# A linear-attention block and an MLP on one core: other zero products, another engine for the finest level of the first two tiles, 128 weight columns at three levels of the first tile, and another order

## The chip, the cores and the metric

The kernel runs on 1 core of one Trainium2 chip. The metric is the device time of one execution in microseconds. Three executions of the kernel before took 588.12, 589.46 and 591.12 us; the median is 589.46. One more execution was profiled; it took 589.61 us, of which the trace spans 587.8. All durations below are from that one.

## The reference

The attention is a recurrence over time with a decay per channel; its output, laid out as tokens by channels, goes through an MLP with the exact gelu.

```python
# r, k, v, w: (4, 8, 768, 48), u: (8, 48)
for t in range(S):
    cur = np.einsum('bhd,bhe->bhde', u[None] * kt, vt)
    y[:, :, t] = np.einsum('bhd,bhde->bhe', rt, state + cur)
    state = wt[:, :, :, None] * state + np.einsum('bhd,bhe->bhde', kt, vt)
x = y.transpose(0, 2, 1, 3).reshape(3072, 384)
h = x @ w_in                      # (384, 2048)
out = (0.5 * h * (1.0 + erf(h / sqrt(2)))) @ w_out   # (2048, 384)
```

Activations are 32-bit floats; the two weight matrices arrive as 64-bit floats.

## The kernel before

**Tiles.** The work is cut into 8 tiles x = 0 to 7: four batches by two halves of 384 time steps. A tile has all 8 heads, two to a slot of the partitions (g = 0, 1, 64 partitions each, 48 used). `attention(x, unit)` makes a tile's xT (channels by 384 steps), `mlp(x)` turns it into output rows. Tile 0's attention runs as two parts (units, np_ = 1) that alternate; later tiles have one. The loads of r, k, w (`rkw`) and v of a tile come by SP's queue.

**Inside a chunk of 64 steps** the attention needs the 64x64 matrix of k·r products with the decays between the two times. It is built in `a_sb` (k's time on partitions, r's time along the row, chunks c = 0, 1 on the two halves of the partitions) by levels h = 1, 2, 4, 8, 16, 32. At level h the products of a later block of h steps with the block of h steps before it are valid. Tiles 0 and 1 do it with `halves()`, tiles 2 to 7 with `quarters()`, which the diff does not touch. In `halves()`, for each h:

- `products` (L443 to L456) fills a pair of PSUM banks `d` by PE, with 64x64 weights on four 64x64 tiles of the array, 24 matmuls (each 2 records in the trace, and 2 of PEld) in a part of tile 0, 48 in tile 1. In tile 0 two products of zeros, 128x128 by 512, follow (`keep_warm(2)`).
- At h = 1 the diagonal's products with u·r (`diagonal`, in `kx` by ACT, L401) come next.
- DVE multiplies r and k by the decays for the next level (L494 in separate halves, L505 in one instruction). It needs that level's products done, since it overwrites their input.
- The result goes from `d` to the places of `a_sb` where the level is valid: for h below 16 by DVE's COPY_PREDICATED with a mask (L516), for h = 16 and 32 by ACT copies of blocks of 16 or 32 rows (L513). At h = 1 DVE then copies the diagonal by a mask (`copy_diagonal`, L465).

There are three pairs of banks `d`, so a product of a later level waits until an earlier pair has been copied.

**Then** k is transposed (kt_ps L685, copied by ACT L687), k·v per chunk (kv_ps L711), DVE chains the states (L731, L726), PE adds to y the part inside the chunk (L752) and that of the states (L797), with a small DVE copy between them (`fence`, L762 and L764), and DVE and ACT copy y to xT (L804, L820, and over `ysb` L823 and DMAs L827).

**MLP.** Tile 0's MLP has 16 column blocks of three 128x384 matmuls (L1059) with gelu by ACT in two banks, and then the products with w_out (L1153). Tiles 1 to 7 use a form with sums of blocks (L929, L1073), and POOL issues adding DMAs there (L980).

**Weights** come in 16 pieces of 64-bit numbers (`raw`, five buffers) and are turned to 32 bits by three ACT passes (L333, L334, L336) and two DVE instructions, a shift (L345) and an add (L349). The first MLP's block pair n needs piece n. `weight_in` issues a piece's load; some loads are held back until DVE has done a one-element memset of their target (L204, and L163 for tile 1's r, k, w).

**Order.** Nothing is scheduled by a tool: each part of the work is a generator, and the strings in `PLAN` say, letter by letter, which generator runs to its next yield. Engines execute their own instructions in the order in which this issues them. In `PLAN[0]` "." and "s" are the two parts of tile 0, "f" is tile 1's attention, "c" the weights' conversion, "l" loads. In `PLAN[x]` "." is the MLP of tile x - 1, "s" and "f" the attentions of tiles x and x + 1.

At the start `keep_warm(8)` (L225) issues eight products of zeros while the first loads run, and masks for h = 1, 2, 4, 8 and the diagonal are made by DVE.

Of the kernel before, what the change touches and what calls it, by code (L numbers as in the profile page):

```python
# [10 lines left out]
F32 = mybir.dt.float32  # L11
# [17 lines left out]
NI = Q * N3  # L29
LEVELS = (1, 2, 4, 8, 16, 32)  # L30
QUARTERS = (4, 16)
FINE = 4
BANK = 512
# [3 lines left out]
NC_SP = 8  # L37
HALFWAY = 2
PLAN = {
    0: "l.s....llsl.lssslslss.lc.l.slslls...ssss..lcs.s.s.l.ss..ss..sccs.c.s.llpssslw..cs.ffpcc",  # L40
    1: (
        "..ccswccc.csl.scscs.s.sccwsc.clccs.ccsccc.csc.lscclswwclc.scs.wcssw.ss.cclcsc.ccs.lclccsc."
        "ccclfccccccfccfcccccfccfccwf.ff......fw.sl.w.x.wx...x..x...xww"
    ),
    2: (
        "s.s.....ss....ssw.ws.wl.wsss.wws.s..lsl...lws.w..s.ww....s.s..l..sss.lssss....s..s..s.sls."
        "llsf.sf.fs..fl.xx.x.fxx"
    ),
    3: (
        "ls.ls....lss..ss.....ss..l.s.lsss.sss.s.s.s.ss..sss..sssssss....s.s..l...s..l.sslslsf.ffs."  # L50
        "..x.lx..xxx"
    ),
    4: (
        "lls.s.sss..s.l.........ssss.....sss.s.ss.s..s.sllss...s.s..l.sss.ss..s.ss...s..sslsll.s..f"
        ".sf.sf..ff..xx.xflxx"
    ),
    5: (
        "..ss...s..ssl....sls...s.sss..sss..sss.sls...sllss..sssss.s..l..s.s...s.slll..s.ssfsf.fsf."
        "....xxx.lxx"
    ),  # L60
    6: (
        "ss..sss...s.....s.sl..s...l.s.ssls.s.s..s..sssssl......ss.ssss.sl.sl...s.....ss..llsssl.f."
        "s.fsf.f.f.xx.l.xffxx"
    ),
    7: "....ss.s...s.s.s....s.sss..ss.ss.sss..s..sss..sssssss......s.s....s..ssss.s...x.x..xxx",
}


# [5 lines left out]
def kernel(  # L74
# [31 lines left out]
    def pair(name):  # L106
        return pools["d"].tile([128, 2, BANK], F32, name=name, tag="d")
# [116 lines left out]
        for _ in range(n):  # L224
            nc.tensor.matmul(t, lhsT=zeros[:, 0:128], rhs=zeros, start=True, stop=True)  # L225

    keep_warm(8)


    masks = {h: const.tile([128, C // 2], U8, name=f"mask{h}") for h in LEVELS if h < 16}  # L230
# [9 lines left out]
    for h in masks:  # L240
        if not h:
            continue
        sh = h.bit_length() - 1
        s_h = s_qs.get(h, s_t)
        nc.vector.tensor_scalar(out=s_h, in0=row, scalar1=sh, scalar2=None, op0=ALU.logical_shift_right)
        nc.vector.tensor_scalar(out=m_h[:, 0:C // 2], in0=col[:, 0:C // 2], scalar1=sh, scalar2=1,
                                op0=ALU.logical_shift_right, op1=ALU.logical_shift_left)
        nc.vector.tensor_tensor(out=masks[h], in0=s_h[:, 0:C // 2], in1=m_h[:, 0:C // 2], op=ALU.is_equal)
# [58 lines left out]
    def conversion():  # L307

        i = converted[0]
        if i >= len(pieces):  # L310
            return
        converted[0] += 1

        prepare(i + HALFWAY if i > 1 else 0)
        yield
        if wide:
            yield from finish(pieces[i][0], raws[i], *halfway[i])
        for _ in weight_in(i + 3):
            pass

    def convert():
        for _ in conversion():
# [30 lines left out]
    def attention(x, unit):  # L353
# [91 lines left out]
        def products(bs, right, width, rest=False):  # L445
            d = pair("d")
            n = 0
            for b in bs:
                for i in range(NI):
                    for g in range(2):  # L450
                        for p in range(2):
                            nc.tensor.matmul(d[half[p], g, n * width:(n + 1) * width],  # L452
                                             lhsT=kc[half[g], b, i, p], rhs=right(half[g], b, i, p),
                                             start=True, stop=True)
# [14 lines left out]
        def halves():  # L469

            for h in LEVELS:
                m = C // 2 // h
                if np_ < NPART:

                    d = products(range(np_), lambda z, b, i, p: rc[z, b, i, p], C, h == 1)
                    d = d.rearrange("p g (n m two j) -> p g n m two j", two=2, j=h, m=m)[:, :, :, :, 1, :]
                else:
                    right = rc.rearrange("p b i c (m two j) -> p b i c m two j", two=2, j=h)[:, :, :, :, :, 1, :]
                    d = products(range(np_), lambda z, b, i, p: right[z, b, i, p], C // 2)
                    d = d.rearrange("p g (n m j) -> p g n m j", j=h, m=m)  # L480
# [10 lines left out]
                tt = bass.AP(tensor=t2.tensor, offset=t2.offset, ap=[t2.ap[0], [1, 2]] + list(t2.ap[1:]))  # L491

                def update(z, r2=r2, t2=t2, k2=k2, tk=tk):
                    nc.vector.tensor_mul(*((k2, k2, tk) if z is k else (r2, r2, t2)))  # L494

                if x == 0 and m == 1:

                    update(k)
                    last_r.append(lambda: update(r))
                elif x == 0 and h == 1:  # L500
                    update(r)
                    yield
                    update(k)
                else:
                    nc.vector.tensor_mul(rk, rk, tt)  # L505
                yield
                ah = at.rearrange("p g n (m two j) -> p g n m two j", two=2, j=h)[:, :, :, :, 1, :]
                if h >= 16:

                    for p in range(2):  # L510
                        for i in range(m):
                            s = slice(p * 64 + i * 2 * h, p * 64 + i * 2 * h + h)
                            nc.scalar.copy(out=ah[s, :, :, i], in_=d[s, :, :, i])  # L513
                else:
                    mask = masks[h].rearrange("p (m j) -> p m j", j=h).unsqueeze(1).unsqueeze(1)
                    nc.vector.copy_predicated(out=ah, mask=mask.to_broadcast(ah.shape), data=d)  # L516
                if h == 1:
                    copy_diagonal(diag)
                yield
# [798 lines left out]
```

## Time and profile before

| what | value |
|---|---|
| median of three executions | 589.46 us |
| profiled execution | 589.61 us, span 587.8 us |
| PE busy | 571.1 us, 97% of the span |
| DVE busy | 425.5 us, 72% |
| ACT busy | 291.2 us, 50% |
| POOL busy | 58.6 us, 10% |
| first MLP matmul of tile 0 (L1059) starts | 44.40 us |
| output products of tile 0 done, banks of tiles 1 to 7 set up (L115) | 118.36 us |

The span begins with the first instruction. "PE" rows are matmuls, "PEld" the loads of their weights. A row of the timeline gives start, length, engine, line, operation, output and input, how many instructions were merged, and in brackets the idle time before and what ended it; "issue" means that nothing the profile shows was waited for. A busy PE is not a PE at its peak: matmuls are pipelined, and a row of merged matmuls holds the last one's whole latency.

### The profile page before, as it was taken

The page shows a single profiled execution, that of the slowest core. Times are in us where ns is not written, and L with a number is a line of the kernel's source. Part 1 is how long each engine was busy: PE and PEld are TensorE (multiplying, and loading weights), DVE is VectorE, ACT ScalarE, POOL GpSimd, SP SyncE. Part 2 cuts the span into 40 slices and gives each one's busy share as a digit, 9 for nine tenths or more (in the row PEclk, how much of TensorE's full clock was granted, in tenths as well). Part 3 has the DMA queues.
Part 4 walks back from the last instruction along what each step waited for, and adds up shares of the span by engine and source line. Part 5 has one row for each costly group of instructions (what it writes and reads, how often), then busy time and mean ns, then how long its engine had stood idle before and what let it go on. Part 6 is the DMA issues. An engine that isn't in the chain of part 4 may idle for free. (4 is left out here: it accounts for less than half of the span.)

```text
span 587.8 us, 17656 instructions
## 1 busy us (share of the span) xinstructions
PE 571.1 (97%) x7602; PEld 521.4 (89%) x7616; DVE 425.5 (72%) x825; ACT 291.2 (50%) x668; POOL 58.6 (10%) x63
## 2 busy tenths in 40 slices
PE   5789999999999999999999999999999999999997
PEld 3576666799999999999999999999998999999997
DVE  5988968989758975777959986777759987420332
ACT  2368898446362567235462467245561467335400
POOL 3100000013000130012000130002100111003100
PEclk8999999999999999999999999999999999999999
DMA  6749742253032542354122632344224333114201
GB/s 230 221 135 352 265 168 78 79 142 52 5 89 64 157 58 41 90 142 93 26 55 79 151 70 44 86 139 74 27 41 119 86 42 42 29 45 55 28 13 35
DMA packets 62430, 55.09 MB, mean 94 GB/s; under 512 B 32400, under 2 KB 47504, under 8 KB 62352
## 3 DMA queue, kind: packets, MB, share of 16 engines
q1 hardware_dynamic: 50832, 45.62, 25.5%
q0 software_dynamic: 11424, 8.26, 10.8%
q8 instruction: 60, 0.98, 0.7%
q14 instruction: 18, 0.15, 0.1%
q10 hardware_dynamic: 96, 0.07, 0.1%
HBM read 36.24 MB, written 4.72 MB: 70 GB/s over the span
## 5 line engine op out<-in xcount | busy, mean ns | idle before, releaser
L929 PE MATMUL h_ps<-xT,w_in_sb 128*128 128x192 f32 x560 | 111.5, 330 | 0.6 <-DVE o_sb L1196 0.6
L980 POOL DMA_DIRECT2D g<-o_sb x42 | 50.6, 1229 | 478.2 <-ACT o_sb L965 468.9
L929 PEld LDWEIGHTS h_ps<-xT,w_in_sb 128*128 128x128 f32 x560 | 93.0, 190 | 4.7 <-ACT g L961 1.6
L929 PE MATMUL u_ps<-s,w_in_sb 128*128 128x192 f32 x224 | 41.2, 327 | 0.0
L1073 PE MATMUL o_ps<-w_out_sb,g 128*128 128x192 f32 x224 | 39.8, 326 | 0.0
L929 PEld LDWEIGHTS u_ps<-s,w_in_sb 128*128 128x128 f32 x224 | 37.1, 190 | 0.2
L1073 PEld LDWEIGHTS o_ps<-w_out_sb,g 128*128 128x128 f32 x224 | 37.0, 190 | 0.0
L604 ACT COPY a_sb<-d 32x256 f32<-32x256 f32 (+8 forms) x90 | 32.6, 362 | 4.9 <-PE d L588 3.4
L1059 PE MATMUL h_ps<-xT,w_in_sb 128*128 128x384 f32 x96 | 33.2, 494 | 0.0
L452 PEld LDWEIGHTS d<-rkw 64*64 64x64 f32 x1152 | 19.4, 138 | 14.7 <-issue 10.5
L1073 PE MATMUL o_ps<-w_out_sb,f 128*128 128x192 f32 x176 | 32.0, 331 | 0.0
L1073 PE MATMUL o_ps<-t,g 128*128 128x192 f32 x176 | 31.4, 330 | 0.0
L1073 PE MATMUL o_ps<-t,s 128*128 128x192 f32 x176 | 31.2, 328 | 0.0
L1073 PE MATMUL o_ps<-t,e 128*128 128x192 f32 x176 | 30.6, 326 | 0.5 <-issue 0.5
L621 DVE COPY_PREDICATED a_sb<-quarter,d 128x480 f32<-128x480 uint8 (+5 forms) x54 | 23.2, 439 | 10.5 <-PE d L588 9.3
L726 DVE SCALAR_TENSOR_TENSOR st<-st,tot_sb,kv_ps 128x48 f32<-128x48 f32 x160 | 28.9, 258 | 2.6 <-PE kv_ps L711 2.5
L1073 PE MATMUL o_ps<-w_out_sb,e 128*128 128x192 f32 x176 | 30.7, 328 | 0.0
L982 DVE TENSOR_TENSOR g<-g,o_sb 128x384 f32<-128x384 f32 x14 | 7.6, 549 | 31.2 <-ACT o_sb L965 31.1
L1073 PEld LDWEIGHTS o_ps<-t,e 128*128 128x128 f32 x176 | 28.9, 190 | 0.7 <-issue 0.7
L1073 PEld LDWEIGHTS o_ps<-t,g 128*128 128x128 f32 x176 | 28.6, 190 | 0.5
L1073 PEld LDWEIGHTS o_ps<-w_out_sb,f 128*128 128x128 f32 x176 | 28.5, 190 | 0.6
L1073 PEld LDWEIGHTS o_ps<-t,s 128*128 128x128 f32 x176 | 28.8, 190 | 0.2
(163 smaller groups left out, 1171.3 us busy)
## 6 DMA issues: line engine op xcount, KB each, us to landing
rkw<-in_rkw_dram SPq DMA_DIRECT2D x54, 256.0 KB, 3.6
g<-o_sb POOLq DMA_DIRECT2D x42, 192.0 KB, 3.6
raw<-in_w_out_dram SPq DMA_DIRECT2D x8, 768.0 KB, 6.2
v_in<-in_v_dram SPq DMA_DIRECT2D x8, 584.0 KB, 4.6
raw<-in_w_in_dram SPq DMA_DIRECT2D x5, 768.0 KB, 7.5
out_dram<-o_sb SPq DMA_DIRECT2D x20, 192.0 KB, 2.0
rkw<-kx SPq DMA_DIRECT2D x72, 48.0 KB, 2.0
rkw<-in_rkw_dram SPq DMA_DIRECT2D x6, 384.0 KB, 6.2
```

The lines of the kernel that those rows point to most:

```text
L452: nc.tensor.matmul(d[half[p], g, n * width:(n + 1) * width], lhsT=kc[half[g], b, i, p], rhs=right(half[g], b, i, p), start=True, stop=True)
L604: nc.scalar.copy(out=at[z, g, first:behind, (a + 1) * h:], in_=d[z, :, :, to] if g == slice(None) else d[z, :, to])
L621: nc.vector.copy_predicated(out=an[:, :, :, :, (a + 1) * h:], mask=mask.to_broadcast(data.shape), data=data)
L726: nc.vector.scalar_tensor_tensor(out=stq[:, q, c], in0=stq[:, q, c - 1] if c else b4[:, q, NC - 1], scalar=totq[:, q, c:c + 1], in1=kvs[q ...
L929: nc.tensor.matmul(o, lhsT=lhsT, rhs=rhs, start=start, stop=True, skip_group_check=True)
L980: nc.gpsimd.dma_start(out=g, in_=z, accum_op=ALU.add)
L982: nc.vector.tensor_add(g, g, z)
L1059: nc.tensor.matmul(h_ps, lhsT=w_in_sb[:, f // FI, j, f % FI * 128:(f % FI + 1) * 128], rhs=xT[:, j, :], start=(j == 0), stop=(j == NJ - 1))
L1073: nc.tensor.matmul(o, lhsT=lhs(j), rhs=rhs(j), start=start and j == 0, stop=(j == HF - 1), skip_group_check=True)
```

## The change

Five edits.

1. The opening burst of zero products goes from 8 to 24.
2. The two zero products after each set of tile 0 become four on 64x64 tiles, each with 512 columns (`keep_warm_tiles`).
3. In tile 0, levels 1, 16 and 32 use `products_of_both`: weights of both chunks of a pair side by side, 64 rows by 128 columns, and as moving data the later blocks of both chunks, 64 columns. 12 matmuls take the place of 24; half of the result is used.
4. At h = 1, in tiles 0 and 1, ACT copies the products to all odd columns of `a_sb` (two copies of 64x384 per part of tile 0, one of 128x768 in tile 1), and POOL sets those with k's time after r's to zero by two affine selects of 64 partitions (384 columns in tile 0, 768 in tile 1). DVE's mask for h = 1 and its COPY_PREDICATED are gone. The coarser levels overwrite the rest.
5. All strings of `PLAN` are other strings. Weight piece 3 is loaded beside piece 4 after the second conversion, where it was loaded after the first.

In the order that results, the load of the first third of weight piece 0 is released after DVE's first update of r instead of before the first loads have landed. In tile 0 one part's transposes stand before the other part's products of h = 32, the shift of weight piece 0 before the updates of h = 8 and its add before the last update, and the shift of piece 1 before the last fence. In tile 1 the MLP matmuls of tile 0 between the products of successive steps, from h = 1's diagonal to h = 2, 4, 8, 16, 32 and the transposes, are 9, 6, 3, 3, 6 and 3, where they were 6, 6, 6, 6, 6 and 3. PE's instructions of tiles 1 to 7 are the same in number and shape.

```diff
 PLAN = {
-    0: "l.s....llsl.lssslslss.lc.l.slslls...ssss..lcs.s.s.l.ss..ss..sccs.c.s.llpssslw..cs.ffpcc",
+    0: ".s...ls.lsl.l.sslsls.ls.s..llcss.lclslsc.slsslcl..ls.ss.sc.lss...s.sp...sscs.wc.ss.ccfpf",
...
-    keep_warm(8)
+    def keep_warm_tiles():
+        ts = [ps.tile([128, BANK], F32, name="warm", tag="mm", bufs=2) for _ in range(2)]
+        for p in range(2):
+            for g in range(2):
+                nc.tensor.matmul(ts[g][half[p]], lhsT=zeros[half[g], 0:64], rhs=zeros[half[g]], start=True, stop=True)
+
+    keep_warm(24)
...
-        for _ in weight_in(i + 3):
-            pass
+        for n in (() if i == 0 else (3, 4) if i == 1 else (i + 3,)):
+            for _ in weight_in(n):
+                pass
...
             if x == 0 and not rest:
-                keep_warm(2)
+                keep_warm_tiles()
             return d[:, :, 0:n * width]
+
+        def products_of_both(h):
+            odd = rc.rearrange("p b i c (m two j) -> p b i c m two j", two=2, j=h)[:, :, :, :, :, 1, :]
+            d = pair("d")
+            for i in range(NI):
+                for g in range(2):
+                    nc.tensor.matmul(d[:, g, i * C:(i + 1) * C], lhsT=kc[half[g], 0, i].rearrange("p c t -> p (c t)"),
+                                     rhs=odd[half[g], 0, i], start=True, stop=True)
+            keep_warm_tiles()
+            return d[:, :, 0:NI * C].rearrange("p g (n c m j) -> p g n c m j", c=2, j=h, m=C // 2 // h)
...
-                if np_ < NPART:
+                if x == 0 and (h >= 16 or h == 1):
+                    d = products_of_both(h)
+                elif np_ < NPART:
...
+                if h == 1:
+                    if x == 0:
+                        for p in range(2):
+                            nc.scalar.copy(out=ah[half[p]], in_=d[half[p], :, :, p])
+                    else:
+                        nc.scalar.copy(out=ah, in_=d)
+                    for z in half:
+                        a1 = ah[z, :, :, :, 0]
+                        nc.gpsimd.affine_select(out=a1, in_=a1, pattern=[[0, 2], [0, a1.shape[2]], [2, m]], base=1,
+                                                channel_multiplier=-1, compare_op=ALU.is_ge, fill=0.0)
...
-                            nc.scalar.copy(out=ah[s, :, :, i], in_=d[s, :, :, i])
-                else:
+                            nc.scalar.copy(out=ah[s, :, :, i], in_=d[s, :, :, p, i] if x == 0 else d[s, :, :, i])
+                elif h > 1:
                     mask = masks[h].rearrange("p (m j) -> p m j", j=h).unsqueeze(1).unsqueeze(1)
                     nc.vector.copy_predicated(out=ah, mask=mask.to_broadcast(ah.shape), data=d)
```

More of the change, by code (lines that the diff above doesn't have):

```diff
@@ L225, in keep_warm @@
             nc.tensor.matmul(t, lhsT=zeros[:, 0:128], rhs=zeros, start=True, stop=True)
-    keep_warm(8)
-    masks = {h: const.tile([128, C // 2], U8, name=f"mask{h}") for h in LEVELS if h < 16}
+    def keep_warm_tiles():
[4 more added lines that the diff above has]
+    keep_warm(24)
+    masks = {h: const.tile([128, C // 2], U8, name=f"mask{h}") if h > 1 else None for h in LEVELS if h < 16}
     masks[0] = const.tile([128, C], U8, name="mask0")
@@ L245 @@
         nc.vector.tensor_scalar(out=s_h, in0=row, scalar1=sh, scalar2=None, op0=ALU.logical_shift_right)
+        if h == 1:
+            continue
         nc.vector.tensor_scalar(out=m_h[:, 0:C // 2], in0=col[:, 0:C // 2], scalar1=sh, scalar2=1,
@@ L506, in halves @@
                 yield
-                ah = at.rearrange("p g n (m two j) -> p g n m two j", two=2, j=h)[:, :, :, :, 1, :]
                 if h >= 16:
```

28 lines of the change are left out of this document (15 added, 13 removed).

## The prediction

> **What bounds the kernel now.** I read the page, then the busy time by stretch, then the timelines of PE, DVE, ACT and POOL in the first 120 us, then the waits. The stretches are tile 0's attention, its MLP beside tile 1's attention, and the rest:
>
> ```profile
> 0.00:44.40 44.40, 32.59 (x1078) 24.15 (x1092) 34.60 (x106) 17.75 (x32) 7.99 (x21) 0.96 0.62 196
> 44.40:118.40 74.00, 74.00 (x1070) 49.38 (x1069) 64.39 (x106) 57.46 (x95) 0.00 (x0) 1.00 0.53 186
> 118.40:588.00 469.60, 464.47 (x5458) 447.83 (x5457) 326.53 (x614) 216.04 (x543) 50.64 (x42) 1.00 0.32 69
> ```
>
> Columns: stretch, length, busy us of PE, PEld, DVE, ACT, POOL, then clock, DMA share and GB/s. From 44.40 on PE has no gap to speak of: 74.00 of 74.00, then 5.1 us idle, 3.1 of them the tail after its last matmul, so 2.0 us that another order could win back. The change leaves PE's instructions of tiles 1 to 7 the same in number and shape. So it can gain by making the first MLP product start before 44.40, and lose by making PE wait after it. Before 44.40 DVE is the engine in front:
>
> ```profile
> 12.33 0.56 DVE L494 TENSOR_TENSOR rkw<-rkw 128x384 f32<-128x384 f32 x1 [0.66 <-PE d L452]
> 12.83 1.02 DVE L516 COPY_PREDICATED a_sb<-mask,d 128x384 f32<-128x384 uint8 x1
> 13.89 1.02 DVE L465 COPY_PREDICATED a_sb<-mask,d 128x768 f32<-128x768 uint8 x1
> ...
> 15.78 1.02 DVE L516 COPY_PREDICATED a_sb<-mask,d 128x384 f32<-128x384 uint8 x1
> 16.83 1.02 DVE L465 COPY_PREDICATED a_sb<-mask,d 128x768 f32<-128x768 uint8 x1
> 17.76 0.95 DVE L505 TENSOR_TENSOR rkw<-rkw,tot_sb 128x768 f32<-128x768 f32 x1
> ```
>
> The two L516 here are the finest level that leaves DVE. PE's own part is the clock, and two gaps marked issue (1.42 us at 21.09, 0.96 at 37.43):
>
> ```profile
> 2.29 3.59 PE L225 MATMUL warm<-zeros 128*128 128x512 bf16 x8 [2.29 <-ACT zeros L217]
> 9.43 1.56 PE L452 MATMUL d<-rkw 64*64 64x64 f32 x48 [3.55 <-DMA rkw<-in_rkw_dram]
> 10.74 1.54 PE L452 MATMUL d<-kx,rkw 64*64 64x64 f32 x48
> ...
> 13.00 0.93 PE L452 MATMUL d<-rkw 64*64 64x64 f32 x48
> ```
>
> A set of products takes 1.56 at 9.43 and 0.93 from 13.00; by stretches the granted clock is 0.51 from 9.3 to 12.8 and 1.00 after.
>
> **Part 1, up to the end of h=1 in tile 0.** The opening burst grows from 8 to 24. Slow ones start 0.425 apart (weight loads 2.70, 3.12, 3.55); fast ones 0.216 (the five at 43.09: 1.47 less 0.39 of its own, by 5). If the clock opens 3.5 us after the burst begins, 8 slow and 16 fast take 6.9 us and end at 9.2, just before k lands (9.4); opening one stretch later, 10.8; never, 12.5. I take 9.2, as the 0.51 stretch was also one of 3.5 us of work. [...]
> The two first sets then take 0.93 each, and DVE's second update starts at 11.5, not 12.33. In place of L516 come two ACT copies of 64x384 per part (0.48 each, like L804's 48x384) and two POOL selects. ACT is done with u·r at 11.4, so the first part's copies end at 12.35. **The selects have one row**: an affine select of 128 columns took 0.29. Memsets of 1536 columns in 1.38 and of 128 in about 0.28 split into 0.16 fixed and 0.0009 a column; so split, the select of 384 columns is 0.55, and of 768 (tile 1) 0.93; plainly scaled 0.87 and 1.74; at the rate of POOL's strided copies (0.44 for 128 columns) 1.32 and 2.64. I take 0.55 and 0.93, the same operation, and keep the copies' rate as the far end; there is no near end below the memset's. Two run one after the other, ending at 13.2.
> The diagonal copy (L465) writes over what the selects wrote, and in the new order waits for the second select; DVE is in order, so the second part's updates, h=2 and everything else of tile 0 queue behind it. So it runs from 13.2 to 14.2 where it ended at 14.91: 0.7 of the 1.02 is kept. The second part: updates to 15.25, its selects done by then, diagonal to 16.25, against 17.85: 1.6 ahead.
> One row speaks against selects beside DVE:
>
> ```profile
> 16.94 2.05 POOL L289 COPY rkw<-ident 32x128 f32<-32x128 f32 x3
> ```
>
> Two of these three take 0.44 each; the third, which began at 17.86, inside DVE's multiplication of 17.76, took 1.13. [...]
>
> **Part 2, h=2 to the last state.** h=2 keeps its 3.7 us of DVE. h=4 had a 0.47 wait behind the first issue gap; a weight's shift (L345, 0.55) is now before h=8. So h=16 starts at 26.2, not 27.69: 1.5 ahead. There PE alternates with DVE, sets 1.40 apart (28.09, 29.48, 30.88), of which 0.53 are two zero products; four on 64x64 tiles cover the array once, so about 0.3. The sets of h=16, 32 and 1 become 24 instructions with 128 columns of weights on two 64-row tiles instead of 48 on four. Bounds: the same spacing per instruction gives 0.6; no overlap of the two tiles, at the transposes' 0.109 ((1.47-0.27)/11), 2.8. I take 0.95, as array time is unchanged and the 64x64 rows show tiles running side by side. For the last h=32, one part's transposes (0.75) are now ahead, and ACT's eight copies of 16 rows (0.37 each) must be done: update at 30.6, not 31.88. Behind it stood shift 0.55 and add 0.96 of a weight; the add is now in an earlier PE wait, so the first state copy is at 32.15, not 34.94: 2.8 ahead. State chains 1.84 each, the shift before the fence 0.55: the second part's last products begin at 37.35, not 40.04. From there to 44.40 PE ran gapless (products, six zero products, first MLP). **Lead at the first MLP product: 2.7**; I take 2.4, since an issue gap may again meet the chain. Bounds 0.9 (selects at the copies' rate put the first diagonal 1.5 later) and 3.2 (no gap; the weight piece that ran with the first loads, 256 KB of 3.2 MB before 12 us, is now asked for later, so k lands up to 0.4 earlier). The other moved weight loads (piece 3 beside piece 4, behind xT's) are needed about 9 us after issue, against 7.5 to landing.
>
> **Part 3, tile 1.** Its h=1 goes the same way: DVE loses 1.88, ACT gains a 128x768 copy (0.80, like L687), POOL two selects of 768, and DVE's diagonal waits for both. The order asks more of PE: between the products of h=4, 8 and 16 stand three MLP matmuls where there were six. Count from the first MLP matmul. ACT: u·r to 1.0, a weight's three passes to 4.0, gelu to 4.6, copy to 5.4. POOL: 5.5 to 7.4. DVE: update to 5.5, **idle to 7.4**, diagonals 1.96, shift and add of weight piece 2 to 10.8, piece 3 to 12.6, update of h=2 1.76 to 14.4, then shift 0.5, copy 1.87, add 0.96, shift 0.5, update of h=4 to 20.0. PE: h=2 products end at 11.4, six MLP matmuls 4.14, h=4 products to 17.15, three matmuls to 19.2, then it waits for 20.0: **0.8 lost**. Nothing covers this, as PE is the bound. With selects of 1.74 it loses 2.3 (1.1 of it at piece 2), with 2.64 4.2, below 0.6 nothing.
>
> **Part 4, tiles 2 to 7.** Other orders, the same work. One tile's products with the states now follow those inside the chunk with no output product between (it was 0.65): 0.2 for the fence. Between losing some such gaps and winning half of the 2.0 I take plus 0.2.
>
> **Sum**, against the profiled execution's 589.61 (span 587.8; the median shown is 589.46, 0.15 away): 589.6 - 2.4 + 0.8 + 0.2 = **588.2**.
>
> **Rivals.** (a) Slower: DVE behind POOL's selects. At the copies' rate: lead 0.9, loss 4.2: 589.6 - 0.9 + 4.2 + 0.2 = 593.1; the sign turns at about 1.6 us for a select of 768. For it: POOL's only strided row; against: the select's own row is 0.29 for 128. 0.20. (b) Selects of 0.6 or less, no issue gap on the chain, half the later idle won: 589.6 - 3.0 - 1.0 = 585.6. For it: DVE's 64.39 of 74.00 leave room; against: the shorter distances between levels. 0.20. (c) 128-column sets that don't overlap: about 1.8 on the first and on each of two late sets, of which the first hides 1.0: 589.6 - 2.4 + 4.4 + 0.8 + 0.2 = 592.6. Against it: four tiles do overlap. 0.08. (d) The change doesn't do what it says: the burst stays slow to 12.5 and holds the first products back; full clock only afterwards. Lead 0.3: 590.3. 0.10. Forecast: 0.42.
>
> **Chances.** 0.5% (2.9 us) is about what a measurement of this kernel can tell from no change: the limits are 586.5 and 592.4. Faster: (b) and a little of the forecast, 0.24. Slower: most of (a), half of (c), 0.16. Same 0.60. Range 585.4 to 592.4: it leaves out the end of (b) and the far part of (a) and (c).
>
> **What would show it.** First MLP product near 42.0 (lead); clock 1.00 at the first set and its length near 0.95; the diagonal's wait named POOL, ending near 13.2; selects of 0.55 and 0.93; a PE gap of about 0.8 before h=8's products in tile 1; PE in 118 to 588 with 2 us idle besides the tail. It is wrong if the selects are slower, if issue gaps move onto the chain, or if the clock falls again where the zero products shrink.

## The result, and the profile after

The changed kernel took 597.17 us (median of 6 executions, 595.15 to 600.44) against 588.27 for the kernel before on the same chip: ratio 1.0152, 95% interval 1.0114 to 1.0189. It is slower by 1.5%, outside the predicted range. The profiled execution is the fastest of the six, 595.15 us with a span of 593.4. Three times of PE, the engine that bounds both kernels, split the difference:

| profiled execution | before | after, predicted | after, measured |
|---|---|---|---|
| first MLP product starts | 44.40 | 42.0 | 44.81 (+0.41) |
| from there to the banks line L115 | 73.96 | +0.8 | 77.70 (+3.74) |
| from there to PE's last end | 466.46 | +0.2 | 467.92 (+1.46) |
| what follows PE's last end | 4.79 | | 4.72 |
| time | 589.61 | 588.2 | 595.15 (+5.54) |

The busy time of after by the same three stretches (columns: stretch, length, busy us of PE, PEld, DVE, ACT, POOL, clock, DMA share, GB/s):

```profile
0.00:44.81 44.81, 36.29 (x995) 27.44 (x996) 33.42 (x104) 21.38 (x38) 7.97 (x20) 1.00 0.64 199
44.81:122.51 77.70, 74.87 (x1069) 49.61 (x1068) 61.12 (x105) 56.78 (x93) 6.00 (x7) 1.00 0.50 174
122.51:593.40 470.89, 464.75 (x5460) 448.06 (x5457) 327.15 (x611) 216.21 (x543) 50.71 (x42) 1.00 0.33 69
```

The second row tells most: PE had no gap there before (74.00 of 74.00) and now stands for 2.8 us; the other 0.9 us are a longer busy time for the same work, 0.34 of it in one set (1.94 us at 64.45, where others take 1.60), the rest not traced. PE's timeline of after shows the pieces (columns: start, length, engine, line, operation, tiles, count, and the idle time ahead with what ended it):

```profile
2.36 7.22 PE L225 MATMUL warm<-zeros 128*128 128x512 bf16 x24 [2.36 <-ACT zeros L217]
9.51 1.56 PE L476 MATMUL d<-rkw 64*128 64x64 f32 x24
...
28.27 1.55 PE L476 MATMUL d<-rkw 64*128 64x64 f32 x24
...
39.40 1.32 PE L832 MATMUL y_ps<-rkw,st 64*64 64x64 f32 x38 [0.98 <-DVE fence L797]
...
43.50 1.47 PE L225 MATMUL warm<-zeros 128*128 128x512 bf16 x6 [1.35 <-issue]
...
64.45 1.94 PE L462 MATMUL d<-rkw 64*64 64x32 f32 x96 [0.72 <-DVE rkw L541]
...
71.75 0.66 PE L462 MATMUL d<-rkw 64*64 64x32 f32 x28 [2.05 <-issue]
```

The burst ends at 9.58 and the clock is full from the first set (granted 1.00 from 9.5 to 44.8 us). But a set with 128 weight columns takes 1.56 us, as long as one of 48 instructions took in before at a granted clock of 0.51 (9.43). Two gaps are marked issue: no engine and no transfer that the profile names held PE. DVE's and POOL's timelines of after, for the selects and the end of the first tile:

```profile
12.18 0.56 DVE L530 TENSOR_TENSOR rkw<-rkw 128x384 f32<-128x384 f32 x1 [0.44 <-PE d L462]
13.23 1.03 DVE L486 COPY_PREDICATED a_sb<-mask,d 128x768 f32<-128x768 uint8 x1 [0.47 <-POOL a_sb L526]
...
26.33 0.94 DVE L541 TENSOR_TENSOR rkw<-rkw,tot_sb 128x768 f32<-128x768 f32 x1
28.05 0.96 DVE L541 TENSOR_TENSOR rkw<-rkw,tot_sb 128x768 f32<-128x768 f32 x1 [0.78 <-PE d L476]
29.87 0.56 DVE L530 TENSOR_TENSOR rkw<-rkw,tot_sb 128x384 f32<-128x384 f32 x1 [0.87 <-PE d L476]
32.95 1.50 DVE L530 TENSOR_TENSOR rkw<-rkw,tot_sb 128x384 f32<-128x384 f32 x3 [1.65 <-PE d L476]
34.37 0.25 DVE L766 COPY st<-kv_ps 128x96 f32<-128x96 f32 x1
...
48.59 1.76 DVE L541 TENSOR_TENSOR rkw<-rkw 128x1536 f32<-128x1536 f32 x1 [3.05 <-ACT a_sb L523]
52.30 1.92 DVE L486 COPY_PREDICATED a_sb<-mask,d 128x768 f32<-128x768 uint8 x2 [1.95 <-POOL a_sb L526]
```

```profile
11.75 0.58 POOL L526 TENSOR_SCALAR_AFFINE_SELECT a_sb<-a_sb 64x384 f32<-64x384 f32 x1 [4.03 <-ACT a_sb L521]
12.40 0.79 POOL L526 TENSOR_SCALAR_AFFINE_SELECT a_sb<-a_sb 64x384 f32<-64x384 f32 x1
...
48.62 2.58 POOL L526 TENSOR_SCALAR_AFFINE_SELECT a_sb<-a_sb 64x768 f32<-64x768 f32 x1 [32.62 <-ACT a_sb L523]
51.27 1.00 POOL L526 TENSOR_SCALAR_AFFINE_SELECT a_sb<-a_sb 64x768 f32<-64x768 f32 x1
```

At the first h=16 update (26.33; forecast 26.2) the first tile was where the forecast had it. From there DVE waits 0.78, 0.87 and 1.65 us for the 128-column sets, the last products with the states begin at 39.40 instead of 37.35, and the issue gap of 1.35 us uses up the rest of the lead.

**By the times of its packets, the gaps marked issue are PE waiting for its own instructions.** The page lists a DMA queue named instruction, with 59 packets of 16 KB:

```profile
q8 instruction: 59, 0.97, 0.7%
```

PE's 15,040 matmuls and weight loads are 255 for each packet. By the trace's records of that queue one packet begins at 68.57 us, while the set of h=16 runs, and takes 1.90; PE executes 120 more records and stands still until 71.75, 3.18 after the packet began. The one that begins at 41.06 takes 0.96: 116 records, and the gap ends 2.44 after its start. In before the packets between 42.8 and 75 us begin at 42.76, 50.4, 57.4, 62.8, 67.3 and 74.6, at ends of sets or within MLP products, where the next 118 records take 2.58 to 6.00 us, longer than the 2.32 and 2.34 us that pass from a packet's start to the end of before's gaps at 21.09 and 37.43; there is no gap there. I call theory T1: where a block ends decides whether PE waits, and any added instruction shifts all ends behind it. The rivals: T2, DVE behind POOL's selects; T3, the 128-column sets; T4, half clock behind idle windows; T5, the new orders of tiles 2 to 7.

### The profile page after: what moved, and what is told of

Its sections match the earlier page's. It is cut to its first block, busy times and chain, and to the rows that moved or that the text cites. A ratio compares the mean times of both kernels' runs of the same rounds, so it can differ in the third digit from the quotient of the medians.

```text
span 593.4 us, 17489 instructions
## 1 busy us (share of the span) xinstructions
PE 575.9 (97%) x7520; PEld 525.1 (88%) x7520; DVE 421.7 (71%) x820; ACT 294.4 (50%) x673; POOL 64.7 (11%) x69
## 3 DMA queue, kind: packets, MB, share of 16 engines
HBM read 36.24 MB, written 4.72 MB: 69 GB/s over the span
## 4 chain that ended last, share of the span: by engine, by line
PE 58%; DVE 7%; DMA 1%; issue 0%; ACT 0%; SPq 0%; DVEq 0%
PE o_ps L1108 25%; PE h_ps L964 13%; PE u_ps L964 12%; PE d L623 4%; DVE rkw L429 2%; DVE kx L395 2%; PE y_ps L832 1%; PE kv_ps L746 1%; PE y_ps L787 1%; DVE st L761 1%; DVE rkw L388 1%; DMA rkw<-in_rkw_dram 1%; DMA xT<-ysb 1%; DVE kx L401 1%; PE d L614 0%
## 5 line engine op out<-in xcount | busy, mean ns | idle before, releaser
L1108 PEld LDWEIGHTS o_ps<-w_out_sb,e 128*128 128x128 f32 x176 | 28.8, 190 | 0.2
```

Of the source, the lines that this page charges most:

```text
L1108: nc.tensor.matmul(o, lhsT=lhs(j), rhs=rhs(j), start=start and j == 0, stop=(j == HF - 1), skip_group_check=True)
```

## The experiments

All kernels compute the full output. Run names begin with the kernel they start from: b before, a after, c a mixture. The last four columns are of the profiled execution: first MLP product, from there to the banks line, from there to PE's last end, and the waits marked issue between 8 and 50 us. That execution can lie well off the median (a_mask1's took 598.40, b_phase256's 593.29, b_zeros0's 592.01). And b_zeros4 and b_zeros4_again are one kernel: their profiles differ by 2.16 us at the first MLP product and by 0.4 and 0.8 in the next two columns. A smaller difference in these columns alone shows little.

| run | us | ratio to before, interval | first MLP | to L115 | to end | issue |
|---|---|---|---|---|---|---|
| before | 588.2 to 589.5 | 1 | 44.40 | 73.96 | 466.46 | 3.2 |
| after | 597.17 | 1.0152, 1.0114 to 1.0189 | 44.81 | 77.70 | 467.92 | 1.3 |
| b_phase160 | 593.02 | 1.0070, 1.0040 to 1.0100 | 47.71 | 75.54 | 465.18 | 5.9 |
| b_phase256 | 590.48 | 1.0022, 1.0002 to 1.0042 | 48.09 | 74.56 | 465.83 | 5.1 |
| a_phase144 | 594.91 | 1.0098, 1.0067 to 1.0128 | 46.69 | 75.84 | 467.84 | 2.7 |
| a_mask1 | 594.57 | 1.0099, 1.0062 to 1.0136 | 46.36 | 79.18 | 468.15 | 1.6 |
| a_phase144_mask1 | 594.82 | 1.0099, 1.0073 to 1.0124 | 46.89 | 75.86 | 467.92 | 2.7 |
| a_64cols | 594.12 | 1.0078, 1.0052 to 1.0103 | 45.28 | 76.26 | 467.43 | 4.3 |
| a_orders | 593.90 | 1.0077, 1.0041 to 1.0113 | 46.85 | 76.78 | 465.34 | 1.5 |
| a_orders_phase164 | 591.68 | 1.0053, 1.0030 to 1.0076 | 45.18 | 79.19 | 464.93 | 0 |
| a_later_orders | 592.39 | 1.0046, 1.0025 to 1.0067 | 47.06 | 76.27 | 465.05 | 2.1 |
| a_zeros2 | 594.23 | 1.0078, 1.0050 to 1.0106 | 46.04 | 75.56 | 467.73 | 0 |
| b_selects | 594.85 | 1.0109, 1.0046 to 1.0172 | 43.70 | 78.31 | 466.18 | 3.0 |
| b_selects_tile0 | 589.60 | 1.0026, 1.0007 to 1.0044 | 44.29 | 73.96 | 466.64 | 2.4 |
| b_cols128 | 590.51 | 1.0018, 1.0000 to 1.0036 | 45.02 | 74.38 | 465.64 | 0.9 |
| b_zeros4 | 588.07 | 0.9980, 0.9954 to 1.0006 | 44.18 | 74.67 | 464.92 | 4.5 |
| b_zeros4_again | 587.66 | 0.9978, 0.9954 to 1.0003 | 42.02 | 75.09 | 465.75 | 2.9 |
| b_zeros0 | 588.66 | 0.9981, 0.9966 to 0.9996 | 46.78 | 74.55 | 465.87 | 6.6 |
| c_first_tile_64 | 590.53 | 1.0039, 1.0020 to 1.0058 | 47.97 | 74.69 | 465.09 | 7.5 |
| c_zeros4_selects_tile0 | 592.82 | 1.0052, 1.0022 to 1.0082 | 48.13 | 74.49 | 465.49 | 7.7 |

**Where the blocks end: b_phase160, b_phase256, a_phase144.** The opening burst is cut into more and smaller products of zeros; the diff is that of b_phase160, b_phase256 has 136 of 30 columns, and a_phase144 has 96 of 128 columns (with 128 weight columns) in place of `keep_warm(24)`:

```diff
-    keep_warm(8)
+    burst = ps.tile([128, BANK], F32, name="warm", tag="mm", bufs=2)
+    for _ in range(88):
+        nc.tensor.matmul(burst[0:48, 0:46], lhsT=zeros[:, 0:48], rhs=zeros[:, 0:46], start=True, stop=True)
```

> The kernel before, with its opening burst of 8 products of zeros of 512 columns made of 88 small ones (48 weight columns, 46 columns): about as many columns, but 160 more PE instruction records ahead of everything. Nothing else differs. Theory T1 (PE's instructions arrive in blocks of 256; PE runs dry when a block ends inside a dense set of products, since a set uses up 192 records in about 1.6 us): the blocks' ends move by 160 records, so that some of them fall into products of tile 1, and the trace shows 2 to 5 new gaps of 0.7 to 2 us marked issue after 44 us; the kernel is 2 to 6 us slower than before (about 591 to 594). The rival, that where a block ends does not matter and the after kernel lost its time to DVE, POOL and the 128-column sets alone: within 0.7 us of before (588 to 589), no new gaps.

> The kernel before with its opening burst of 8 products of 512 columns made of 136 small ones (48 weight columns, 30 columns), that is 256 more PE records, one whole block. T1: the blocks end where they did in before, so from the first MLP product to the first line of the rest (L115's first transpose) it takes 74.0 us as there, and the whole time is within 0.9 us of before, the first tile's own scatter. The rival, that small products or added records cost by themselves whatever the phase: slower by at least as much as the run with 160 more (3.8 us).

> The kernel after, with its opening burst of 24 products of 512 columns made of 96 products of 128 columns: as many columns, 144 more records. T1: the gaps of 1.35 us at 43.5 and 2.05 us at 71.75 go (others of less may come), and the time falls 2 to 3.4 us below that of after. The rival (those gaps come from something that the change does to DVE, ACT or POOL): both gaps stay where they are, time as after within 0.7.

160 records more cost 3.8 us (593.02 against 589.23 beside it), 256, about a whole block by the 254 and 255 records a packet of before and after, 1.6 (590.48 against 588.86). T1 expected nothing for the latter; the direction is right, the distance is not clean. That small products in the burst cost time by themselves is no better account: b_zeros4 and b_zeros0 have such bursts too and lie below the kernel before. Nor do the gaps lie where I had expected them: b_phase160 has one of 1.04 us behind 44 us, and most of its gaps in the first tile, the longest 2.69 us ahead of 41.16; two windows of half clock stand behind them (granted 0.93 from 9 to 44 us). In a_phase144 both gaps of after are gone and the stretch to L115 falls from 77.70 to 75.84, as expected; the median falls by 2.3. But a gap of 2.31 us now stands in the first tile, and the clock halves behind it. PE's timeline and the busy time by stretch of a_phase144:

```profile
16.32 0.86 PE L464 MATMUL d<-rkw 64*64 64x64 f32 x42
19.48 0.28 PE L464 MATMUL d<-rkw 64*64 64x64 f32 x3 [2.31 <-issue]
```

```profile
17.30:20.70 3.40, 1.22 (x62) 1.15 (x62) 1.97 (x5) 2.87 (x3) 0.00 (x0) 1.00 0.87 255
20.70:24.10 3.40, 2.39 (x59) 1.42 (x52) 3.38 (x7) 0.00 (x0) 0.00 (x0) 0.50 0.09 30
24.10:27.50 3.40, 3.06 (x103) 2.88 (x104) 3.15 (x12) 0.00 (x0) 0.00 (x0) 0.50 0.82 248
```

The set stops behind its 42nd of 48 matmuls, so no data was missing. A window with 2.18 of 3.40 us idle is followed by two at clock 0.50.

**The selects: a_mask1, a_phase144_mask1, b_selects, b_selects_tile0.** The first two give tile 1's finest level back to DVE (the diff; the second with a_phase144's burst). The last two put the block from `if h == 1` to `fill=0.0` of the change into the kernel before, for both tiles or, with `and x == 0`, for the first alone.

```diff
-                if h == 1:
+                if h == 1 and x == 0:
...
-                elif h > 1:
+                elif h > 1 or x:
                     mask = masks[h].rearrange("p (m j) -> p m j", j=h).unsqueeze(1).unsqueeze(1)
```

> The kernel after, with the finest level of tile 1 taken back to DVE (its mask made again, one copy under the mask of 128x768 in place of the ScalarE copy and the two selects); PE's instructions are unchanged, so its blocks end where they did. Theory T2 (DVE behind the selects costs PE its waits in tile 1): the wait of 1.95 us on the diagonal goes, a copy of 1.88 comes back, and the 0.72 us gap before the products of h=8 stays or shrinks by 0.1: the selects in tile 1 are worth 0 to 0.3 us. [...]

> The run a_phase144 (594.91; no issue gaps in tile 1) with the finest level of tile 1 taken back to DVE. T2: DVE's 1.88 us copy comes back and its wait of 1.95 us for POOL goes; the gap of 0.87 before the products of h=8 stays within 0.2, time 594.4 to 595.4. Rival (the prediction's step that POOL's selects cost PE 0.8 us there): the gap goes and 594.0 or less.

> The kernel before with the finest level's copy moved to ScalarE and GpSimd's selects (tile 0 and 1), nothing else; PE's records are those of before, so its blocks end where they did. T2 (the selects, locked out while DVE multiplies, take back what DVE's shorter list gives): the first diagonal's copy ends 0.3 to 0.8 us earlier than 14.91, in tile 1 DVE waits 1.5 to 2 us for POOL; first MLP product 0.3 to 1.0 us earlier than 44.40, tile 1 as long as it was; 588.4 to 589.5. The rival of the prediction (DVE behind the selects makes PE wait in tile 1 by 1 us or more): 590 to 592.

> The kernel before with the finest level by ScalarE and GpSimd in the first tile alone; tile 1 keeps DVE's copy under a mask. If the 5.3 us that both tiles' selects cost came from tile 1 (in the old order ScalarE's copy stands behind two weight pieces, 55.05 us, and the products of h=4 wait 2.24 us for it), the time falls to 588 to 589.5, the first MLP product stays near 43.7 and the stretch from there to L115 is 74.0 to 74.7. Rival (the first tile's selects do harm later): 591 or more.

With equal block ends (a_phase144 and a_phase144_mask1) tile 1's selects are worth nothing: 594.91 and 594.82, the gap before h=8 0.87 and 0.81, as expected. The 2.6 us by which a_mask1 lies below after I don't credit to them: its gap before h=8 is 0.82, and in its profile the clock halves twice (granted 0.993 over the run). In the kernel before, however, the same edit costs 6.0 us (594.85 against 588.86), which I had not expected, and some 5.2 of it is tile 1's (589.60 without). The timeline of b_selects, all engines:

```profile
54.12 1.06 ACT L338 ACTIVATE e<-raw 128x768 f16<-128x768 f32 x1
55.05 0.80 ACT L502 COPY a_sb<-d 128x768 f32<-128x768 f32 x1
...
55.90 1.60 PE L454 MATMUL d<-rkw 64*64 64x32 f32 x96 [2.24 <-ACT a_sb L502]
55.97 2.05 POOL L505 TENSOR_SCALAR_AFFINE_SELECT a_sb<-a_sb 64x768 f32<-64x768 f32 x2 [35.70 <-ACT a_sb L502]
...
58.06 1.02 DVE L467 COPY_PREDICATED a_sb<-mask,d 128x768 f32<-128x768 uint8 x1 [6.63 <-POOL a_sb L505]
```

Two weight pieces stand ahead of the copy in ACT's order, and it begins at 55.05, when the last pass over them (54.12, 1.06 long) ends; the copy frees the bank pair that PE's next products need, and these wait 2.24 us for it. The changed order puts it at 47.63, ahead of these pieces: edit and order of tile 1 belong together. In the first tile the selects bring the first state copy from 34.94 to 34.02; behind it a gap of 1.45 us marked issue takes the gain (first MLP product 44.29), and 589.60 is at the upper end of what was expected.

**128 weight columns: a_64cols, b_cols128.** a_64cols takes `products_of_both` out again; b_cols128 puts it into the kernel before for h=16 and 32.

```diff
-                if x == 0 and (h >= 16 or h == 1):
-                    d = products_of_both(h)
-                elif np_ < NPART:
+                if np_ < NPART:
```

> The kernel after, with the products of h=32, 16 and 1 in the first tile made again of 48 instructions on 64x64 tiles in place of 24 with 128 weight columns (the four zero products stay). Theory T3 (a set with 128 weight columns takes 1.56 us where one of 64 takes 0.93, and the late ones stand on the chain with DVE): those sets fall to 0.9 to 1.0 each, and the second part's last products, at 39.40 us in after, begin at 37.3 to 37.8. Rival (the late sets are hidden behind DVE or ACT): they begin at 39.0 to 39.5. For the whole time T1 has a say too, as 288 records more move the ends of the blocks by 32: the sets alone would give 1.6 to 2 us less than after.

> The kernel before with the products of h=16 and h=32 in the first tile made with 128 weight columns (24 instructions of 64x128 instead of 48 of 64x64), the burst made of 104 products of 40 columns so that the records before the first MLP product are as many as in before. T3 (such a set takes 1.56 us in place of 0.93, three of them on the chain with DVE): the sets are 2.0 to 2.1 us apart instead of 1.40, the second part's last products 1.2 to 1.9 us later than 40.04; 590 to 591.5. The prediction's own step (0.95 a set, no loss): at 40.0 or earlier, 588.5 to 589.5. A third outcome: half as many records per set spare PE an issue gap there, and the loss is 0.5 or less.

In b_cols128 the sets stand 2.02 us apart instead of 1.40, with no gap inside; PE's timeline:

```profile
27.17 1.55 PE L468 MATMUL d<-rkw 64*128 64x64 f32 x24
28.66 0.61 PE L225 MATMUL warm<-zeros 128*128 128x512 bf16 x2
29.19 1.55 PE L468 MATMUL d<-rkw 64*128 64x64 f32 x24
30.68 0.60 PE L225 MATMUL warm<-zeros 128*128 128x512 bf16 x2
```

The last products begin at 40.94 instead of 40.04, less than the 1.2 to 1.9 of T3; the time, 590.51, is in its range. In a_64cols the unbroken sets are 0.93 long again, and yet the last products begin at 39.99, later than in after: neither T3's 37.3 to 37.8 nor the rival's 39.0 to 39.5. PE's timeline of a_64cols:

```profile
25.70 0.50 PE L462 MATMUL d<-rkw 64*64 64x64 f32 x17 [0.22 <-DVE rkw L539]
27.79 0.63 PE L462 MATMUL d<-rkw 64*64 64x64 f32 x28 [1.58 <-issue]
```

A 64x64 set uses 96 records in 0.93 us, one with 128 columns 48 in 1.56. Among the quicker sets stand waits marked issue (4.3 us between 8 and 50 us, 1.3 in after), and a window of half clock followed (granted 0.997 over the run). So the 128-column sets cost their length and spare gaps. In b_cols128 that costs 0.90 us at the last products, and 1.0 in the median, with an interval that just reaches 1. In after the two about cancel by the first MLP product (45.28 without these sets, 44.81 with them); that a_64cols is 3.05 us faster than after in the median is not theirs alone, as the ends of its blocks moved too and its gap in tile 1 is 0.79 where after's is 2.05.

**Orders: a_orders, a_orders_phase164, a_later_orders.** `PLAN[1]` to `PLAN[7]`, or `PLAN[2]` to `PLAN[7]`, of before in the changed kernel (a_later_orders with the burst of a_phase144, and one more "s" ahead of `PLAN[2]`).

> The kernel after with the orders of tiles 1 to 7 of before; the first tile keeps its new order, and all else stays changed. Theory T5 (the new orders of tiles 1 to 7 lose 1.5 us in tiles 2 to 7 and, with three MLP products in places between levels, 0.7 us in tile 1): from L115's first transpose to PE's end 466.5 us instead of 467.9, the gap before the products of h=8 gone. T1: its blocks end 91 records away (modulo 256) from where before's do, so that one or two of them still fall into products of tile 1, for 1 to 2 us. Together 590.5 to 593; without T1 (T5 alone) 589 to 590.5; if the orders do not matter 594 to 597.

> The same with the opening burst of 24 products of 512 columns made of 106 products of 116 columns, 164 records more, which brings the ends of the blocks to where they lie in before, counted from the first MLP product. T1: from there to L115's first transpose 73.9 to 74.4 us, and less than in the run without the added records by the gaps that it shows; whole time 588.5 to 590.5, the same as before. Rival (phase does not matter): the same as the run without them within 0.7.

> The kernel after with the burst of 96 products of 128 columns (the run a_phase144, 594.91) and the orders of tiles 2 to 7 of before; the first tile and tile 1 keep the new orders. Theory T5: the new orders of tiles 2 to 7 cost 2.5 us, as L115's first transpose to PE's end took 467.8 us in a_phase144, and 465.3 and 464.9 in the two runs that had the old orders of tiles 1 to 7. So that stretch takes 465 to 466, first MLP product to L115 stays near 75.8 us, and the time is 592 to 593.2. Rival (that stretch became shorter for another reason, the end of tile 1's order): 594 to 595.5.

a_later_orders and its partner a_phase144 differ in nothing else: 592.39 against 594.91, and the last stretch 465.05 against 467.84. T5 holds, at 2.5 to 2.8 us. The table agrees: that stretch takes 467.43 to 468.15 in the six runs with the new orders of tiles 2 to 7, 464.92 to 466.64 in the fourteen with the old. PE's waits in the last stretch, of after and then of a_later_orders (columns: us in total, times, longest):

```profile
PE d L623 <- DVE kx L598: 1.1, 2, 0.6
PE y_ps L832 <- DVE fence L799: 1.0, 2, 0.8
PE y_ps L787 <- DVE st L761: 0.6, 2, 0.3
PE h_ps L964 <- DVE o_sb L1231: 0.5, 2, 0.3
```

```profile
PE h_ps L948 <- DVE o_sb L1215: 0.4, 2, 0.2
PE y_ps L771 <- DVE st L745: 0.3, 1, 0.3
PE d L607 <- DVE kx L582: 0.3, 1, 0.3
```

3.2 us against 1.0, so these waits make up 2.2 of it. The run a_orders came out above its 590.5 to 593 (593.90). In a_orders and a_orders_phase164 the last stretch is short too (465.34, 464.93), but tile 1 waits 1.70 and 1.88 us for ACT's copy, as in b_selects; and 6.8 us at half clock follow in a_orders_phase164, which so missed its 588.5 to 590.5, although it shows no wait marked issue up to 50 us.

**Zero products: a_zeros2, b_zeros4, b_zeros4_again, b_zeros0.** The diff is that of b_zeros4, timed twice; a_zeros2 is the reverse in the changed kernel, and b_zeros0 has no products of zeros there. The bursts of small products make the numbers of instructions equal (b_zeros4: 108 of 38 columns, one block more).

```diff
             if x == 0 and not rest:
-                keep_warm(2)
+                keep_warm_tiles()
```

> The kernel after with two products of zeros of 128x128 by 512 columns behind each set of the first tile, as in before, in place of four on 64x64 tiles; the burst has 124 products of 99 columns, so that the blocks end where they do in the run a_phase144 (594.91), its partner. Theory T4 (the shorter zeros leave PE more idle behind DVE in the first tile: a window of 3.4 us with over 1.8 us idle is followed by one at half clock, as at 20.0 to 28.6 us in all four runs of that kind, each worth 1 to 1.7 us before the first MLP product): idle per window falls below 1.5, no half clock after the burst, first MLP product 1 to 2 us earlier than the 46.69 there; 593 to 594. Rival (the longer zeros delay the late sets of h=16 and 32 by 0.15 each and win nothing): first MLP product at 46.5 to 47.2, 594.5 to 595.5.

> The kernel before with four products of zeros on 64x64 tiles in place of two of 128x128 behind each set of the first tile; the burst made of 108 products of 38 columns, so that its blocks end one whole block later than in before and as in the run b_phase256 (590.48), its partner. T4: windows of 3.4 us with over 1.8 us idle come, a stretch of half clock between 15 and 32 us, the first MLP product 0.5 to 2 us later; 591 to 592.5. Rival of the prediction (shorter zeros let PE start the next set 0.2 to 0.3 us earlier at h=16 and 32): first MLP product 0.3 to 0.9 us earlier than in before or its partner without fetch gaps; 589.5 to 590.2.

> The kernel before with four zero products on 64x64 tiles (and the small-product burst), timed again. If the 588.07 against 589.51 was a gain, the ratio is again 0.997 to 0.999 and its interval lies below 1; if it was scatter of the first tile, 0.999 to 1.003.

> The kernel before without the products of zeros behind the sets of the first tile; the burst made of 36 products of 114 columns, as many records more as the zeros were. T1 as it now stands (a block of PE instructions can be fetched each 3.3 us or so at best, 2.3 us pass from its start to its first instruction): the 0.53 us of zeros behind each set were time in which blocks came in, and what is won there comes back as gaps marked issue; in the first 40 us these add up to 1 to 3 us more than in before, perhaps with a stretch of half clock, and the first MLP product stays at 44 to 46.5; 588.5 to 591. Rival (the zeros are time on PE's path, 0.53 each on the last five sets): first MLP product at 41.5 to 43, 586 to 587.5.

T4 is half right. With the longer zeros in after no window of half clock and no issue gap is left (granted 1.00 from 9 to 44 us), but the first MLP product comes only 0.65 earlier than in the partner, and the time is 0.7 less, neither clear of the scatter: the sets of h=16 and 32 stand 2.02 us apart there, 1.82 in the partner. In the kernel before the shorter zeros cost nothing, against T4's 591 to 592.5: 0.998 twice, each interval just holding 1, although in b_zeros4 a window of half clock does follow one with 2.1 us without PE. Without any zeros it is the same, 0.9981, though the 0.53 us behind each set are gone. What came in their place is seen in the profiled execution of b_zeros0 (592.01 us, above its median), in PE's timeline:

```profile
33.32 0.90 PE L711 MATMUL kv_ps<-v_in,kx 64*64 64x48 f32 x42
38.36 0.35 PE L711 MATMUL kv_ps<-v_in,kx 64*64 64x48 f32 x3 [4.14 <-issue]
```

**Mixtures: c_first_tile_64, c_zeros4_selects_tile0.** The parts of the first tile without the 128-column sets and with the old orders of tiles 1 to 7; and the two parts that had shown a gain.

> The kernel after without three of its parts: the products with 128 weight columns (64x64 again), the selects in tile 1 (DVE again), the new orders of tiles 1 to 7 (those of before); the burst is made of 103 products of 119 columns so that the blocks end where they do in before. Left are the longer burst, the four zero products, the selects in the first tile, the moved weight loads and the new order of the first tile. Prediction's sum without its 128-column sets: first MLP product at 41.5 to 42.5, then 74.0 and 465.3: 586 to 587.2. T4 (half clock behind DVE's waits in the first tile takes the lead back): first MLP product at 43.5 to 45, 588 to 590.

> The kernel before with four zero products on 64x64 tiles, the finest level by ScalarE and GpSimd in the first tile alone, and a burst of 108 products of 110 columns (as many columns as 24 of 512; the blocks end one block later than in before). The zeros alone gave 588.07, the selects alone moved the first MLP product from 44.40 to 43.70. If the two add: first MLP product at 43.0 to 43.8, then 74.2 and 465.3: 587.0 to 587.9, 1 to 2 us below before. If the selects' gain is lost to half clock (T4): 588 to 589.

Neither gains, and both lie above all that was expected of them. c_first_tile_64 has the first tile that the prediction's sum wanted, and PE's timeline shows what becomes of it:

```profile
13.73 0.63 PE L444 MATMUL d<-rkw 64*64 64x64 f32 x27 [1.61 <-issue]
...
19.48 0.27 PE L444 MATMUL d<-rkw 64*64 64x64 f32 x1 [3.45 <-issue]
...
32.68 0.74 PE L444 MATMUL d<-rkw 64*64 64x64 f32 x34 [1.94 <-issue]
```

7.5 us of waits marked issue and two windows of half clock (granted 0.90 from 9 to 44 us): the first MLP product is at 47.97. c_zeros4_selects_tile0 has 7.7 and 48.13. No version is faster than the kernel before by as much as 0.3%; the nearest is b_zeros4, at 0.9980 and 0.9978.

## Why the prediction was wrong, point by point

- **Burst, clock, first sets.** The burst ended at 9.58 (9.2), the clock was full. But the first set has 128 columns: 1.56, not 0.93, and the second update started at 12.18, not 11.5. The diagonal's copy still began at 13.23 as forecast (13.2), since the selects began at 11.75 ahead of that update and not behind it. That was luck.
- **Selects.** A select of 384 columns took 0.58 where it began ahead of DVE's update and 0.71 to 0.79 where it began during one; of the two of 768 the first, begun at 48.62 beside the update of 48.59 to 50.35, took 2.58, the second 1.00, and in b_selects, where DVE stood idle, each took 0.99 to 1.00. So the chosen sizes (0.55 and 0.93) were about right, and the rest, 1.58 us of it at 48.62, came beside DVE's multiplications; the sum has no term for it. DVE waited 1.95 there for a copy of 1.88 that it no longer did: nothing won or lost, so rival (a) did not happen in this order.
- **128-column sets: the first failed step.** "I take 0.95, as array time is unchanged and the 64x64 rows show tiles running side by side": measured 1.56. The two 64-row tiles did run side by side: by the trace's records the matmuls of a set begin in pairs, 0.007 us apart. But a pair begins 0.116 us after the last one, about as a 128x128 transpose does (0.109), where four 64x64 tiles need 0.063. A set is twelve such steps in either form, so its array time was not unchanged. In these rows the longer step came with the 128 weight columns, while sets of tile 1 that move 32 columns have about the same one as sets that move 64 (0.059 and 0.060; such sets take 1.60 and 1.63 us in before). The bounds (0.6 to 2.8) held the time; rival (c), tiles that do not overlap, at 1.8 more a set, is not what happened, since a set cost 0.6 more. By the last products with the states 2.05 us of the forecast 2.7 were gone. Taking the sets out did not bring them back (39.99 in a_64cols), since waits marked issue came in their place (4.3 us between 8 and 50 us).
- **"I take 2.4, since an issue gap may again meet the chain": the second failed step.** I had put 0.3 on the two issue gaps of before meeting the chain again, and did not ask where they would move. One of 1.35 met the chain directly ahead of the first MLP product; when the ends of the blocks moved (a_phase144), it was gone.
- **Tile 1, "Nothing covers this": 0.8 forecast, 0.72 measured before h=8.** The size came out by luck. ACT's copy ended 3.7 us after the first MLP product instead of 5.4, the selects took 3.6 us instead of 1.9, and so DVE was free of them at 7.5 as forecast (7.4). Nor do the selects cause the gap: with DVE's copy in their place it is 0.81 (a_phase144_mask1), so it belongs to the order. The issue gap of 2.05 at 71.75 was a term that the sum did not have at all, and is the longest gap in after; it too was gone in a_phase144.
- **Tiles 2 to 7: 0.2 forecast, 1.46 measured, 2.5 to 2.8 with all else equal.** I looked at one fence (0.8 instead of 0.2) and set the rest at half lost, half won; the waits sum to 3.2.
- **Median.** The other five executions lie up to 5.3 us above the profiled one. The two slowest show a granted clock of 0.991, and 0.009 of 594 us is 5.3, so half clock can account for the spread. But one with 0.994 is only 0.10 us longer than the profiled one: it depends on where the halved windows fall, and no trace shows that for these executions.

What remains open: 0.9 us of longer busy time in the second stretch; why some blocks begin to load only when PE has run dry (38.73 us in b_phase160, 17.05 in c_first_tile_64, 36.15 in b_zeros0), and so the exact gap of each run. That fetches are late behind other transfers was not tried.

## What to carry to other kernels

In this kernel, with its many small matmuls, PE's instructions are a resource: 0.9 to 7.7 us of waits marked issue stand between 8 and 50 us in 18 of the 20 profiles. Find the queue that carries them, and look whether its packets begin inside dense sets or inside long matmuls. Here 160 PE records more at the start cost 3.8 us and 256 more 1.6, so an edit is to be compared with a partner that has the same number of instructions ahead. And an edit that moves work to an engine with other work queued (ACT here) is only as good as the place that it gets there: in b_selects PE waited 2.24 us for ACT's copy, and the edit cost 6.0 us.

## What the runs showed of the hardware

- **Instruction blocks.** 60 packets of 16 KB in before and 59 in after, for 15,218 and 15,040 matmuls and weight loads of PE: 254 and 255 a packet. No two packets began less than 3.38 us apart in before and 3.32 in after. From a packet's start to the first instruction behind a gap marked issue 2.32 to 2.44 us passed where the transfer took 0.88 to 1.09 (gaps that end at 21.09, 37.43 and 447.61 in before, at 43.50 in after), 3.31 where it took 1.80 (25.60 in before), 3.18 where it took 1.90 (71.75 in after). The waits marked issue were 0.9 to 7.7 us between 8 and 50 us in 18 of the 20 profiles.
- **Clock.** The clock's records in before have one window at half clock while PE works, 9.36 to 12.77, 3.41 us long, behind one in which PE did nothing; from there to PE's end the clock is full, and no window has more than 1.56 us without PE. In after one of 1.74 us (from 16.42) was followed by full clock too. In a_phase144 a window with 2.18 us without PE (17.30 to 20.70) was followed by 6.80 us at 0.50, and in a_later_orders one with 1.91 (18.20 to 21.60) by 6.80 us at 0.50.
- **Tiles.** 24 matmuls of 64 rows by 128 columns on two row tiles took 1.56 us (after, 9.51), 48 of 64x64 on four tiles 0.93 (before, 13.00), for the same products. Both kinds ran side by side; a pair of the first begins each 0.116 us, four of the second each 0.063.
- **A select beside DVE.** In after a GpSimd select of 64x768 took 1.00 us alone (51.27) and 2.58 when it began (48.62) 0.03 us behind a DVE multiplication of two SBUF inputs that lasted 1.76; it ended 0.85 us behind that.
